# Attention, mixer and MLP in one kernel: other tiles for TensorE's transposes, the loads of K, wq and V in one place, another order behind the loop

## The chip, the cores and the metric

The kernel runs on one core of a Trainium2 chip. The metric is the device time in microseconds; lower is better. Before the change three runs gave 1611.37, 1617.12 and 1616.06 us, median 1616.06. The profile is one further execution.

## The reference

An adaptive layer norm block: modulation from `c`, attention of 32 heads against given K and V, then a mixer with an MLP. Cut to what matters (S = 2048 rows, D = 640, 32 heads of 128, F = 1728, all bf16):

```python
mod = (_silu(c) @ w_mod).reshape(c.shape[0], 6, 1, -1)
sa, ca, ga, sb, cb, gb = ...
h = _layernorm(x) * (1 + ca) + sa
q = (h @ wq).reshape(1, 2048, 32, 128).transpose(0, 2, 1, 3)
p = _softmax(einsum('bhqd,bhkd->bhqk', q, k_cache) * 128 ** -0.5)
o = einsum('bhqk,bhkd->bhqd', p, v_cache)
x = x + ga * (o.transpose(0, 2, 1, 3).reshape(1, 2048, 4096) @ wo)
h = _layernorm(x) * (1 + cb) + sb
# mixer: four column groups of the GELU, shifted by 1, -1, 2, -2 rows
t = _gelu(_layernorm(h) @ w1)
x1 = h + shifted(t) @ w2
return x + gb * (x1 + _gelu(_layernorm(x1) @ w3) @ w4)
```

## The kernel before

The kernel writes its whole program as lists of operations, one list for each engine, in the order in which the code issues them; a small class (`Prog`) works out which semaphore waits are needed from the keys that each operation reads and writes. An engine executes its list in order, so the order of the calls is the schedule. DMAs are issued from SyncE's list (and the attention output's stores from GpSimd's).

**The loop (lines 532 to 616).** One step s is one tile of 128 query rows of one head; 16 tiles a head, 32 heads, 512 steps, and 12 more to drain. In step s:

- TensorE computes QK for tile s in two halves of 1024 keys (`qk`, L286), into the PSUM tile `Sps`, and, each behind a QK half, PV in two halves for the tile eight steps back (`pv`, L299; PVD = 8).
- VectorE takes each half out of PSUM with its minimum of the negated scores (L574, into one of three buffers `negS`). GpSimd joins the two minima (L584), and ScalarE computes exp into the ring `Pb` (L587), whose ten slots hold one tile each.
- PV needs the probabilities transposed, in the ring `PTs`. For 14 of the 16 tiles SyncE does it with a DMA transpose from SBUF to SBUF (`transpose`, L222): a pair of tiles in one instruction where the pair is whole, behind the second tile's exp, else a single tile. For the two tiles in `PE_TILES` TensorE does it against an identity matrix (`t_piece`, L253), four transposes behind each PV half, and ScalarE or VectorE copies the result out of PSUM (`t_evac`, L262 and L264).
- Q of the next head is computed a little at a time (`q_piece`, L237): 20 pieces, placed by `QPIECE` in half-steps where no transpose of TensorE stands (`taken`); ScalarE copies it out (`q_evac`, L244).
- For every second tile ScalarE copies the PV result out (L565); GpSimd divides by the row sums (L440, L447) and stores groups of four tiles to DRAM (L454).

`PE_TILES` is (3, 10): tile j is transposed in steps j+3 (first half) and j+4 (second half). VectorE copies the second half of tile 3, ScalarE the other three. Pairs for the DMA are then 0,1; 4,5; 6,7; 8,9; 12,13; 14,15, and singles 2 and 11: eight transposes a head. SyncE's list also has the loads of the next head: K (`load_k`, L205, itself a DMA transpose) in step 2, wq in step 6 (L209), V in step 9 (L214). The last head loads parts of the stored attention output instead (`load_ot`, L497, a DMA transpose), in steps 2 and 9.

**Behind the loop.** `a_pe(j)` (L524) multiplies the attention output of query tile j by wo, over 32 heads; tile 0 is done in three parts, two of them in the loop's drain, ahead of the PV of the tiles at steps NG+PVD-3 and NG+PVD-2 (NG = 512). For each j VectorE then makes the residual and its norm statistics (`a_s1`), the modulated norm (`a_s2`) and the mixer's norm (`nrm_of(1, j)`), two tiles behind one another; GpSimd computes the reciprocal deviations (L624, L626). `n_t(j)` transposes the normed tile on TensorE (L665), ScalarE copies it (L668). `b_op(cc, n)` is one of five column blocks of the mixer's first matmul for 512 rows (L700) with its GELU on ScalarE (L708). `c_op(j)` is the second matmul with its residual (L742, L746). `d_op` and `e_op` are the MLP (L757, L806). `run_fill` puts operations from a list between others.

Of the kernel before, what the change touches and what calls it, by code (L numbers as in the profile page):

```python
# [115 lines left out]
def bass_adaLN_cond__mha_block_cached__mixer_s_mlp__prompt_kernel(  # L116
    nc, A_x, A_k_cache, A_v_cache, A_wq, A_wo, B_x, B_w1, B_w2, B_w3, B_w4, c, w_mod, out,
):
    _, SQ, D = A_x.shape
    _, H, SK, DH = A_k_cache.shape  # L120
    FF = B_w3.shape[1]
    assert DH == 128 and D % 128 == 0 and SQ % 512 == 0 and SK == 2048
    KT = D // 128
    NQT = SQ // 128
# [7 lines left out]
    NG = H * NQT  # L132
# [5 lines left out]
    with ExitStack() as es:  # L138
# [11 lines left out]
        if True:  # L150
            with ExitStack() as es1:
                sb1 = lambda name, shape, dt: es1.enter_context(nc.sbuf_tensor(name, shape, dt))
                RP = 10
                PVD = 8
                PE_TILES = (3, 10)
# [45 lines left out]
                G = Prog(nc, es1, "a")  # L201
# [64 lines left out]
                by_dve = lambda g, r: r == 1 and g % NQT == PE_TILES[0]  # L266

                taken = [u for j in PE_TILES for u in range(2 * (j + 3), 2 * (j + 5))]
# [247 lines left out]
                def a_pe(j, b=None, parts=(0, 1, 2)):  # L516
                    if b is None:
                        b = ybank()
                    pr, z = divmod(j, 2)

                    def f(t):
                        for c0, cw in NC2:
                            for hh in range(OTC[parts[0]], OTC[parts[-1] + 1]):
                                ins = t.matmul(YB[b][:, c0:c0 + cw], OTj[pr % 2][:, 2 * hh + z, :], wo[:, hh, c0:c0 + cw],  # L524
                                               start=(hh == 0), stop=(hh == H - 1))
# [6 lines left out]
                for s in range(NG + PVD + LAG):  # L532
# [10 lines left out]
                    for half in range(2):  # L543
                        if s < NG:
                            qk(s, half)
                        if half == 0 and s in (NG + PVD - 3, NG + PVD - 2):
                            b0 = a_pe(0, None if s == NG + PVD - 3 else b0, (s - NG - PVD + 3,))
                        if 0 <= g_ < NG:
                            pv(g_, half)
                        if s == 0 and half == 1:  # L550
                            q_head0(NQC - 1)
                        if h + 1 < H and 2 * j + half in QPIECE:
                            cc, q = QPIECE[2 * j + half]
                            q_piece(h + 1, cc, q)
# [28 lines left out]
                    if s < NG:  # L583
# [128 lines left out]
                for i in range(NQT + 1):  # L712
                    if i < NQT:
                        b = a_pe(0, b0, (2,)) if i == 0 else a_pe(i)
                        if i >= 3:
                            n_t(i - 3, i == 3)
                        if i == NQT - 3:
                            for z in range(2):
                                G.op("gpsimd", lambda g, z=z: g.memset(us[:, :, z * SQ:z * SQ + 4], 0.0), w=[("usz", z)] + OT0K)
                        if i % 2 == 1 and (i + 3) // 2 < NQT // 2:  # L720
                            load_ot((i + 3) // 2)
# [11 lines left out]
                G.dma("sync", lambda e: e.dma_start(w4[0:FL, NFT - 1, :], B_w4[(NFT - 1) * 128:FF, :]), "w4b", w=["w4b", "wo"])  # L733
                def c_op(j):
# [141 lines left out]
```

## Time and profile before

| | us |
|---|---|
| median of three runs | 1616.06 |
| lowest, highest | 1611.37, 1617.12 |
| the profiled execution, its own time | 1608.0 |
| its span (first to last instruction) | 1606.2 |
| TensorE matmuls, busy | 1488.3 (93%) |
| VectorE, busy | 1394.8 (87%) |
| ScalarE, busy | 1294.5 (81%) |
| GpSimd, busy | 625.0 (39%) |
| the DMA engines moved | 333.60 MB, mean 208 GB/s |
| mean granted clock of TensorE | 0.993 |

How to read the lines below. A line of the groups names a source line, an engine, an operation, output and input tiles with their shapes and the count; then the busy time, the mean length of one in ns, and the idle time of the engine just before them with what ended most of it. A line of the timeline gives the start in us from the span's start, the length, the engine, the source line and the count; in brackets the idle time before and its releaser. PE is TensorE's matmul, PEld its weight load, DVE VectorE, ACT ScalarE, POOL GpSimd, SP SyncE. The loop runs from about 35 to 1259 us of the span, what is behind it to 1606.2.

### The profile page before, as it was taken

To read this page: it belongs to the slowest core of one execution; us is meant where nothing else is said; L and a number is where in the kernel's file an instruction comes from. 1 tells how busy PE (TensorE), PEld (TensorE's weight loads), DVE (VectorE), ACT (ScalarE), POOL (GpSimd) and SP (SyncE) were. 2 spreads that over 40 slices of the span, in tenths; PEclk is the share of its full clock that TensorE was granted. 3 is DMA by queue.
4 is the path that set the end of the run, shared out by engine and by line. 5 is a ranking of instruction groups with operands and counts; after the bars stand their busy time and mean duration, and the time that the engine had idled before them with its cause. 6 is when DMAs were issued, how large, how long until landed. Compare 5 with 4: busy or idle time off the path is not lost.

```text
span 1606.2 us, 34619 instructions
## 1 busy us (share of the span) xinstructions
PE 1488.3 (93%) x13978; PEld 961.6 (60%) x14231; DVE 1394.8 (87%) x2463; ACT 1294.5 (81%) x1145; POOL 625.0 (39%) x1394
## 2 busy tenths in 40 slices
PE   5899999989999999899999999999999799999999
PEld 3466666666666666666666666666666555545444
DVE  6999999999999999999999999999999366656425
ACT  4999999999999999999999999999999400055330
POOL 0244444444444444444444444444444333322000
PEclk9999999999999999999999999999999899999999
DMA  9999999999999999999999999999999995430000
GB/s 308 229 229 237 236 244 236 229 234 251 231 248 247 235 244 240 229 242 237 241 246 241 240 237 233 238 237 246 236 238 241 243 214 106 106 111 1 17 17 34
DMA packets 1167936, 333.60 MB, mean 208 GB/s; under 512 B 1148384, under 2 KB 1161760, under 8 KB 1167776
## 3 DMA queue, kind: packets, MB, share of 16 engines
q1 hardware_dynamic: 1161632, 314.59, 97.1%
q0 software_dynamic: 6144, 16.79, 3.7%
q8 instruction: 112, 1.84, 0.5%
q14 instruction: 48, 0.39, 0.1%
HBM read 43.48 MB, written 19.40 MB: 39 GB/s over the span
## 4 chain that ended last, share of the span: by engine, by line
DVE 36%; PE 22%; ACT 20%; DMA 12%; issue 9%; POOL 1%; POOLq 0%; DVEq 0%
DVE negS L574 33%; ACT ring L587 16%; DMA ring<-ring 12%; PE Sps L524 9%; PE Sps L806 4%; PE Oaug L757 2%; PE QPp L757 2%; ACT ring L262 2%; PE Sps L742 1%; PE PTp L299 1%; ACT kv L244 1%; DVE ring L264 1%; ACT Of L565 1%; PE Sps L286 1%; DVE ring L364 1%
## 5 line engine op out<-in xcount | busy, mean ns | idle before, releaser
L574 DVE TENSOR_SCALAR_CACHE_REDUCE negS<-Sps 128x1024 f32<-128x1024 f32 x1024 | 1178.6, 1221 | 30.0 <-PE Sps L286 29.3
L587 ACT ACTIVATE ring<-negS,small 128x2048 bf16<-128x2048 f32 x512 | 1029.3, 2018 | 22.3 <-POOL small L584 20.7
L299 PEld LDWEIGHTS PTp<-kv,ring 128*128 128x128 bf16 x8192 | 551.9, 98 | 313.9 <-DMA ring<-ring 100.8
L299 PE MATMUL PTp<-kv,ring 128*128 128x129 bf16 x8192 | 647.5, 221 | 52.5 <-DMA ring<-ring 51.8
L286 PE MATMUL Sps<-kv 128*128 128x512 bf16 x1950 | 592.5, 381 | 35.0 <-DVE negS L574 17.2
L584 POOL TENSOR_SCALAR small<-small 128x1 f32<-128x1 f32 x512 | 146.9, 287 | 628.4 <-DVE negS L574 628.3
L286 PEld LDWEIGHTS Sps<-kv 128*128 128x128 bf16 x2048 | 143.2, 97 | 139.4 <-DVE negS L574 94.9
L447 POOL TENSOR_SCALAR On<-Of,small 128x128 bf16<-128x128 f32 x512 | 191.6, 375 | 13.0
L440 POOL TENSOR_TENSOR small<-Of,small 128x4 f32<-128x4 f32 x128 | 133.2, 1041 | 14.6 <-ACT Of L565 14.5
L668 ACT COPY kv<-PTp 128x640 bf16<-128x640 bf16 x32 | 22.0, 692 | 141.1 <-PE PTp L665 141.1
L454 POOL DMA_DIRECT2D o_scratch<-On x128 | 103.1, 806 | 40.8 <-POOL On L447 37.2
L565 ACT COPY Of<-PTp 128x259 f32<-128x259 f32 x256 | 96.2, 376 | 19.6 <-PE PTp L299 19.6
L237 PE MATMUL Oaug<-hTx,kv 128*128 128x512 bf16 x264 | 100.4, 385 | 3.7 <-DVE hTx L396 3.7
L237 PE MATMUL QPp<-hTx,kv 128*128 128x512 bf16 x259 | 97.7, 382 | 2.7 <-ACT hTx L391 2.3
L574 DVE DVE_READ_ACCUMULATOR negS<-Sps 128x1 f32 x1024 | 86.2, 84 | 0.0
L624 POOL TENSOR_SCALAR negS<-negS 128x1 f32<-128x1 f32 x48 | 24.4, 508 | 143.9 <-DVE negS L633 143.9
L638 DVE TENSOR_TENSOR ring<-Sps,mod_bc 128x640 f32<-128x640 f32 x16 | 13.2, 824 | 72.8 <-PE Sps L524 72.8
L524 PE MATMUL Sps<-wo,hTx 128*128 128x512 bf16 (+1 forms) x503 | 70.5, 300 | 0.6 <-issue 0.2
L524 PE MATMUL Sps<-wo,negS 128*128 128x512 bf16 (+1 forms) x505 | 69.3, 298 | 0.4
L810 DVE TENSOR_TENSOR ring<-Sps,ring 128x640 f32<-128x640 f32 x15 | 12.4, 824 | 62.9 <-PE Sps L806 62.8
L262 ACT COPY ring<-Oaug 128x1024 bf16<-128x1024 bf16 x64 | 65.3, 1021 | 0.0
L524 PEld LDWEIGHTS Sps<-wo,hTx 128*128 128x128 bf16 x512 | 40.1, 99 | 31.2 <-issue 1.7
(88 smaller groups left out, 1008.8 us busy)
## 6 DMA issues: line engine op xcount, KB each, us to landing
kv<-in_A_v_cache_dram SPq DMA_DIRECT2D x32, 512.0 KB, 5.0
o_scratch<-On POOLq DMA_DIRECT2D x128, 128.0 KB, 3.8
ring<-in_A_x_dram SPq DMA_DIRECT2D x8, 640.0 KB, 6.4
kv<-in_A_wq_dram SPq DMA_DIRECT2D x32, 160.0 KB, 3.4
wo<-in_A_wo_dram SPq DMA_DIRECT2D x1, 5120.0 KB, 16.4
ring<-ring SPq DMA_TRANSPOSE x256, 7.0
ring<-in_w_mod_dram SPq DMA_DIRECT2D x1, 3200.0 KB, 13.0
out_dram<-wo SPq DMA_DIRECT2D x15, 160.0 KB, 1.8
```

The source lines that it names most:

```text
L237: G.op("tensor", lambda t: t.matmul(JB[jb], wq[:, hb, q, :], hT[:, q, cc * 512:(cc + 1) * 512], start=(q == 0), stop=(q == KT - 1)), r=[(" ...
L262: G.op("scalar", lambda a: a.copy(dst, src), r=[("J", jb)], w=[("PT", g % RP, r)])
L286: ins = t.matmul(Sps[:, col:col + 512], QT[:, hb, j * 128:(j + 1) * 128], KTs[:, hb, col:col + 512], start=True, stop=True)
L299: ins = t.matmul(ob[:, 0:129], PTs[:, b, kt, :], Vaug[:, hb, kt, 0:129], start=(kt == 0), stop=(kt == NKT - 1))
L440: G.op("gpsimd", lambda g: g.tensor_tensor(out=rl[:, 4 * b:4 * b + 4], in0=Of[:].rearrange("p a z d -> p (a z) d")[:, 4 * b:4 * b + 4, 128 ...
L447: G.op("gpsimd", lambda g: g.tensor_scalar(out=On[:, b, z, :], in0=Of[:, 2 * b + z // 2, z % 2, 0:128], scalar1=rl[:, 4 * b + z:4 * b + z ...
L454: G.dma("gpsimd", lambda e: e.dma_start(o_scr[jj // 2:jj // 2 + 2, :, hh].rearrange("a p z d -> p a (z d)"), On[:, b].rearrange("p (a z) d ...
L524: ins = t.matmul(YB[b][:, c0:c0 + cw], OTj[pr % 2][:, 2 * hh + z, :], wo[:, hh, c0:c0 + cw], start=(hh == 0), stop=(hh == H - 1))
L565: G.op("scalar", lambda a, p=p: a.copy(Of[:, p % 4].rearrange("p z d -> p (z d)")[:, 0:259], PO[:, (p % 2) * 512:(p % 2) * 512 + 259]), r= ...
L574: G.op("vector", lambda v, half=half, s=s, r8=r8: v.tensor_scalar(out=negS[:, s % 3, half * 1024:(half + 1) * 1024], in0=Sps[:, half * 102 ...
L584: G.op("gpsimd", lambda g, r8=r8: g.tensor_scalar(out=nm[:, r8:r8 + 1], in0=nm0[:, r8:r8 + 1], scalar1=nm1[:, r8:r8 + 1], scalar2=None, op ...
L587: G.op("scalar", lambda a, s=s, r8=r8: a.activation(Pb[:, s % RP, :], negS[:, s % 3, :], ACT.Exp, bias=nm[:, r8:r8 + 1], scale=-1.0), r=[( ...
```

## The change

In the loop, `PE_TILES` becomes {8: 3, 9: 6}: TensorE transposes tile 8 in steps 11 and 12 and tile 9 in steps 15 and 16, the last of these being step 0 of the next head. DMA transposes are then seven whole pairs. VectorE copies the second half of tile 8 in every head and that of tile 9 in odd heads. `taken`, and so `QPIECE`, follows. K, wq and V are loaded together in step 7, behind the transpose of tiles 6 and 7; the last head's loads of attention output come in steps 5 and 7. Part 0 of the first wo tile moves one step ahead in the drain.

Behind the loop, wo's tiles 14 and 15 are each cut into four parts of eight heads, with mixer blocks and transposes between them (`a_mixed`), and the order of VectorE's work there changes: tile 15's `nrm_of(1, 15)` comes behind `c_op(0)`, its `n_t(15)` behind two more mixer blocks.

```diff
-                PE_TILES = (3, 10)
+                PE_TILES = {8: 3, 9: 6}
...
-                by_dve = lambda g, r: r == 1 and g % NQT == PE_TILES[0]
+                by_dve = lambda g, r: r == 1 and (g % NQT == 8 or g // NQT % 2 == 1)
 
-                taken = [u for j in PE_TILES for u in range(2 * (j + 3), 2 * (j + 5))]
+                taken = [u % (2 * NQT) for j, o in PE_TILES.items() for u in range(2 * (j + o), 2 * (j + o + 2))]
...
-                        if half == 0 and s in (NG + PVD - 3, NG + PVD - 2):
-                            b0 = a_pe(0, None if s == NG + PVD - 3 else b0, (s - NG - PVD + 3,))
+                        if half == 0 and s in (NG + PVD - 4, NG + PVD - 2):
+                            b0 = a_pe(0, None if s == NG + PVD - 4 else b0, ((s - NG - PVD + 4) // 2,))
...
-                            g = s - 3 - r
-                            if 0 <= g < NG and is_pe(g):
-                                t_piece(g, r, half)
-                                if half == 1:
-                                    evacs.append((t_evac, g, r))
+                            for o in PE_TILES.values():
+                                g = s - o - r
+                                if 0 <= g < NG and PE_TILES.get(g % NQT) == o:
+                                    t_piece(g, r, half)
+                                    if half == 1:
+                                        evacs.append((t_evac, g, r))
...
-                        if j == 2 and h >= 1 and h + 1 < H:
-                            load_k(h + 1)
-                        if h + 1 == H and j in (2, PVD + 1):
-                            i = 0 if j == 2 else 1
+                        if j == PVD - 1 and h + 1 < H:
+                            if h >= 1:
+                                load_k(h + 1)
+                            if h + 2 < H:
+                                load_wq(h + 2)
+                            load_v(h + 1)
+                        if h + 1 == H and j in (PVD - 3, PVD - 1):
+                            i = 0 if j == PVD - 3 else 1
                             load_ot(0, OTC[i], OTC[i + 1], i)
-                        if j == 6 and h + 2 < H:
-                            load_wq(h + 2)
-                        if j == PVD + 1 and h + 1 < H:
-                            load_v(h + 1)
...
+                def a_mixed(j, others):
+                    b = None
+                    n = len(others)
+                    for i, fs in enumerate(others):
+                        b = a_pe(j, b, hs=(H * i // n, H * (i + 1) // n))
+                        for fn, x, y in fs:
+                            fn(x, y)
+                    return b
+
-                for i in range(NQT + 1):
-                    if i < NQT:
+                for i in range(NQT):
+                    if i < NQT - 2:
                         b = a_pe(0, b0, (2,)) if i == 0 else a_pe(i)
...
                         a_s1(i, b)
-                        for n in {NQT - 2: (0, 1), NQT - 1: (2, 3, 4)}.get(i, ()):
-                            b_op(0, n)
                     if 1 <= i:
                         a_s2(i - 1)
                     if 2 <= i:
                         nrm_of(1, i - 2)
+                    if i == NQT - 2:
+                        b = a_mixed(i, [[(b_op, 0, 0)], [(b_op, 0, 1)], [(n_t, i - 3, False), (b_op, 0, 2)], [(b_op, 0, 3)]])
+                        a_s1(i, b)
+                    if i == NQT - 1:
+                        b = a_mixed(i, [[(b_op, 0, 4)], [(n_t, i - 3, False), (b_op, 1, 0)], [(b_op, 1, 1)], [(b_op, 1, 2)]])
+                        nrm_of(1, i - 1)
+                        a_s1(i, b)
+                        a_s2(i)
...
+                b_op(1, 3)
+                b_op(1, 4)
                 n_t(NQT - 3, False)
-                nrm_of(1, NQT - 1)
-                for n in range(KT):
-                    b_op(1, n)
                 n_t(NQT - 2, False)
-                n_t(NQT - 1, False)
...
                 for j in range(NQT):
                     c_op(j)
+                    if j == 0:
+                        nrm_of(1, NQT - 1)
                     if j >= 2:
                         n_t(j - 2, False)
-                    run_fill(2)
+                    run_fill(1 if j in (4, 5) else 2)
+                    if j == 0:
+                        n_t(NQT - 1, False)
```

More of the change, by code (lines that the diff above doesn't have):

```diff
@@ L514, in ybank, with a_pe @@
                     return yn[0] % 2
-                def a_pe(j, b=None, parts=(0, 1, 2)):
+                def a_pe(j, b=None, parts=(0, 1, 2), hs=None):
                     if b is None:
@@ L519, in a_pe @@
                     pr, z = divmod(j, 2)
+                    h0, h1 = hs or (OTC[parts[0]], OTC[parts[-1] + 1])
                     def f(t):
                         for c0, cw in NC2:
-                            for hh in range(OTC[parts[0]], OTC[parts[-1] + 1]):
+                            for hh in range(h0, h1):
                                 ins = t.matmul(YB[b][:, c0:c0 + cw], OTj[pr % 2][:, 2 * hh + z, :], wo[:, hh, c0:c0 + cw],
@@ L716, in bass_adaLN_cond__mha_block_cached__mixer_s_mlp__prompt_kernel @@
                             n_t(i - 3, i == 3)
[L717 to L721, printed above, removed]
+                    if i == NQT - 3:
+                        for z in range(2):
+                            G.op("gpsimd", lambda g, z=z: g.memset(us[:, :, z * SQ:z * SQ + 4], 0.0), w=[("usz", z)] + OT0K)
+                    if i % 2 == 1 and (i + 3) // 2 < NQT // 2:
+                        load_ot((i + 3) // 2)
+                    if i < NQT - 2:
                         a_s1(i, b)
-                        for n in {NQT - 2: (0, 1), NQT - 1: (2, 3, 4)}.get(i, ()):
-                            b_op(0, n)
                     if 1 <= i:
```

## The prediction

> **What bounds the kernel now.** I read the slices and the queues of the page first, then the groups of instructions, then SyncE's timeline over one head, then the timelines behind the loop.
>
> ```profile
> DMA  9999999999999999999999999999999995430000
> ...
> q1 hardware_dynamic: 1161632, 314.59, 97.1%
> ...
> L574 DVE TENSOR_SCALAR_CACHE_REDUCE negS<-Sps 128x1024 f32<-128x1024 f32 x1024 | 1178.6, 1221 | 30.0 <-PE Sps L286 29.3
> L587 ACT ACTIVATE ring<-negS,small 128x2048 bf16<-128x2048 f32 x512 | 1029.3, 2018 | 22.3 <-POOL small L584 20.7
> L299 PE MATMUL PTp<-kv,ring 128*128 128x129 bf16 x8192 | 647.5, 221 | 52.5 <-DMA ring<-ring 51.8
> ```
>
> Three resources are nearly full in the loop, and the reader is to see who waits for whom: VectorE (L574) waits for TensorE's QK, TensorE's PV (L299) waits for the transposing DMAs. In numbers per head of 16 steps: the first L574 of step 32 starts at 114.36 us, that of step 496 at 1221.14 us, so 38.16 us a head. VectorE's own need is 32 halves of 1.145 us (start to start in an undisturbed stretch) = 36.64, plus one copy L264:
>
> ```profile
> 667.04 0.69 DVE L264 COPY ring<-QPp 128x1024 bf16<-128x1024 bf16 x1
> ...
> 667.64 1.21 DVE L574 TENSOR_SCALAR_CACHE_REDUCE negS<-Sps 128x1024 f32<-128x1024 f32 x1
> ...
> 682.09 1.02 ACT L262 COPY ring<-Oaug 128x1024 bf16<-128x1024 bf16 x1
> ```
>
> The copy costs VectorE 0.60 (667.64 - 667.04), so its need is 37.24 and 0.92 us a head is waiting, some 28 us over the loop. ScalarE needs 16 exps of 1.905 start to start, 8 copies L565 of 0.26, 4 of L244 at 0.47, 3 of L262 at 0.90: 37.1. Now SyncE's timeline (start, length, line; x counts merged instructions):
>
> ```profile
> 684.82 19.82 SPq L222 DMA_TRANSPOSE ring<-ring  x5
> 704.69 3.35 SPq L205 DMA_TRANSPOSE kv<-in_A_k_cache_dram  x1
> 708.08 4.48 SPq L222 DMA_TRANSPOSE ring<-ring  x1
> 712.60 0.59 SPq L209 DMA_DIRECT2D kv<-in_A_wq_dram  x1
> 713.23 9.23 SPq L222 DMA_TRANSPOSE ring<-ring  x2
> 722.51 0.59 SPq L214 DMA_DIRECT2D kv<-in_A_v_cache_dram  x1
> ```
>
> Each row starts 0.04 us after the one before it ends: the queue never rests, and transposes start 3 to 6 us after the exp they read has ended. So the transfers set the 38.16. From landing to landing (means over 29 heads): pairs 4,5 to 14,15 take 4.11 to 4.28, pair 0,1 5.30, single tile 2 2.41, single 11 2.26, K 2.90, wq 1.28, V 3.24; sum 38.24.
>
> **The change in the loop.** *DMAs.* Singles 2 and 11 become half of pairs 2,3 and 10,11, pair 8,9 falls away. New sum: six pairs at 4.17 + 5.30 + 7.42 for the loads = 37.74, 0.5 less. The bytes stay, so the gain lies between 0 and 0.5 a head; I take 0.5 as the new capacity. By the Trainium skill, DMA: Bandwidth & Descriptors, the cost model, a DMA has a fixed part of about 2 us; if it were paid in line, one DMA fewer would give 2 us a head, 64 in all. The trace speaks against it (two singles take 4.67, a pair 4.17), so it gets no chance of its own.
>
> The loads now come behind pair 6,7. The next pair is ready four steps later (9.16 us); loads and pair take 7.42 + 4.17 = 11.59, so pair 10,11 lands 2.4 us later against its ready time than pair 6,7 does. Today a landing comes about 11 us after ready and PV starts some 0.4 after it; later pairs recover 0.4 each (4.17 in 4.58). K is wanted nine steps (20 us) and V 10 us or more behind their issue, wq a head later: these are covered. V waits for the PV of the last head's tile 15, in the same step 7, done before exp 7 ends: nothing.
>
> *Copies.* VectorE gets tile 8's second half always and tile 9's in odd heads: 1.5 copies a head for 1, +0.30 us, 16 copies x 0.60 = 9.6 us where VectorE sets the pace. ScalarE loses as many; no gain while it waits anyway.
>
> *Tile 9 is transposed late.* Its second half is transposed in step 16 and read by PV half 1 in step 17. In odd heads VectorE copies it right behind its own reduction and PV half 1 waits about 0.3 us, which TensorE makes up. In even heads ScalarE does: exp 14 starts 2.8 us after VectorE's step start (the usual least), exp 15 behind a copy L565 and one L262 at 2.8 + 1.905 - 2.29 + 0.26 + 0.90 = 3.57; the copy of step 16 ends at 3.57 + 1.905 - 2.29 + 1.02 = 4.20, that is 1.91 after step 17 starts. PV half 1 (0.46), a q piece (0.215) and QK of step 18 (0.43) follow: 3.0 to 3.15, where VectorE wants it at 2.29. That is 0.86 us on even heads. Today's steps 13 and 14 carry the same two copies and reach a lag of 4.16 instead of 3.57: the upper bound is 1.45; the lower is 0, if TensorE and VectorE stand in a DMA wait then. I take 0.86, as its inputs are rows of undisturbed steps.
>
> *QPIECE* moves to half-steps 2 to 21; a half-step with one piece takes 1.12 us of TensorE against VectorE's 1.145, and 28 of 32 carry one, before as after: nothing.
>
> *Sum.* VectorE now needs 36.64 + 1.20 = 37.84 in odd heads, 36.64 + 0.60 + 0.86 = 38.10 in even ones, mean 37.97; transfers 37.74. Two near-equal limits with noise (a pair's landing interval scatters by 0.6 to 1.0) give a little more than the larger: some 38.15. **Loop: no change**; bounds -0.4 to +0.7 us a head.
>
> **Behind the loop.** *The drain.*
>
> ```profile
> 1258.61 2.98 PE L299 MATMUL PTp<-kv,ring 128*128 128x129 bf16 x48 [0.17 <-DMA ring<-ring]
> 1266.16 1.92 PE L299 MATMUL PTp<-kv,ring 128*128 128x129 bf16 x16 [4.57 <-DMA ring<-ring]
> ...
> 1270.22 1.92 PE L299 MATMUL PTp<-kv,ring 128*128 128x129 bf16 x16 [2.15 <-DMA ring<-ring]
> ...
> 1272.36 4.32 PE L524 MATMUL Sps<-wo,hTx 128*128 128x512 bf16 x23 [0.22 <-issue]
> ```
>
> TensorE stands 4.6 and 2.2 us for tiles 11 and 12 (single 11 waited behind a load of attention output, 3.60 us of SyncE at 1256.36), and between 1264.4 and 1274.6 its granted clock is 0.50. Tile 0's projection ends at 1284.7, 25.3 us after VectorE's last reduction (1259.4, call it z). New: both loads (3.5 each) come at steps 5 and 7, nothing is between pairs 10,11 to 14,15, so 14,15 is issued at exp 15's end (z+2.8) and lands by z+9. TensorE: tiles 8 to 11 till z+4, part 0 of wo (24 matmuls, 3.4) now ahead of tile 12, tiles 12 and 13 till z+9.4, part 1 till z+12.8, tiles 14 and 15 till z+14.8, part 2 till z+17. **-8.3 us.** Bounds: -2 (only the 2.15 filled) to -10.
>
> What is late next: load_ot(1) (10.94 us of SyncE) must land for tile 2 at z+25.6; it lands at z+21 to 24. load_ot(2) comes behind xt, w1 and w2, and now lands about when tile 4 starts: +0.5 (0 to 2).
>
> *Tiles 14 and 15, the mixer.*
>
> ```profile
> 1427.08 0.45 PE L665 MATMUL PTp<-ident,Of 128*128 128x128 bf16 x5 [2.35 <-DVE Of L656]
> ...
> 1264.40:1274.60 10.20, 6.07 (x38) 4.37 (x40) 0.00 (x0) 0.38 (x1) 3.91 (x7) 0.50 1.20 282
> ...
> 1428.20:1431.60 3.40, 3.40 (x9) 1.22 (x8) 2.61 (x6) 1.21 (x3) 1.03 (x3) 0.50 0.47 100
> ```
>
> (Window rows: bounds, length, busy time by engine, clock, DMA.) Today TensorE waits 2.35 us for VectorE's norm of tile 13, smaller waits 0.7, and 3.4 us at clock 0.50 cost 1.7. The new order takes that wait away, as mixed wo and mixer work covers norms 13 and 14. But tile 15's norm now stands behind a_s1(15), a_s2(15) and c_op(0): 2.8 + 1.7 (GpSimd's rstd) + 2.0 + 1.9 + 0.7 = 9.1 us after the last wo matmul, and TensorE has 6.7 us of work till then (four mixer groups at 1.07, two transposes at 0.45, c_op 1.52): a wait of 2.4 us. If it brings the slow clock as today's 2.35 did, the gain is 0.7; if not, 2.4; if norm 15 comes in time, 4.8; if its chain is 2 us longer, -1.3. I take **-1.2**. By the Trainium skill, TensorE: Matmul & The Clock Gate, HAM oscillation, only idle gaps over some 3.4 us throttle the clock; the row here shows it after 2.35, and the measurement decides. By the rule the gain would be 2.4.
>
> The rest of the tail is TensorE at 99% busy with the same matmuls.
>
> **Sum:** 0 - 8.3 + 0.5 - 1.2 = -9 us. The profiled execution has a span of 1606.2 and a time of 1608.0 (1.8 around it), so 1599 in its terms; it is 8.1 below the median of 1616.06, and I set the difference against the median: **1607**.
>
> **Rivals.**
> - *The transfers alone set the loop (22%).* If the even heads' 0.86 falls into waits that are there anyway, 37.74 rules: -0.41 x 31 = -13, with the tail -22: 1594. For it: today's period is the queue's sum to 0.1 us. Against: VectorE alone needs 37.54.
> - *Tile 9's late copy adds to the DMA waits (22%).* Place: step 17 to 18. If the 0.92 of today stays and 0.30 + 0.43 comes on top, +0.73 x 31 = +22.6, with the tail +14: 1630, slower. It decides as soon as a head takes over 38.46 (9 us of tail over 31 heads). For it: pair 10,11 lands 2.4 us later. Against: a VectorE that stands gives the queue time to catch up.
> - *The tail gives nothing (12%).* load_ot(1) and (2) take the place of the waits: 1615.
> - My forecast, loop unchanged and tail shorter: 44%, 1602 to 1613 by itself.
>
> I call 0.5% (8 us) what can be told from no change. 1607 lies just beyond it: of my own case 26 of 44 points go to faster, with 22 of the first rival 0.48; the rest of it and the third 0.29; the second 0.22 and 0.01 of others slower. The range takes in both rivals' centres: 1592 to 1630.
>
> **What would show it.** Right: seven L222 and one stretch L205, L209, L214 a head; gaps of SyncE behind tile 7; heads of 38.0 to 38.3 us, even ones longer, with L574 waiting in step 18; no wait over 1 us at tiles 11 and 12, and part 0 at full clock; a wait of some 2 us at the transposes (L665) for norm 15. Wrong: a period under 37.8 or over 38.5, or a_pe(2) waiting for its load.

## The result and the profile after

| | before | after |
|---|---|---|
| median, us (22 runs each) | 1611.97 | 1616.24 |
| lowest, highest | 1605.56, 1620.48 | 1608.7, 1623.32 |
| the profiled execution, its time | 1608.0 | 1621.13 |
| its span | 1606.2 | 1619.3 |
| period of a head in the loop (steps 32 to 496, 29 heads) | 38.17 | 38.63 |
| end of VectorE's last reduction, z | 1259.5 | 1277.2 |
| from z to the end of the span | 346.7 | 342.2 |

The ratio is 1.0025, 95% interval 1.0014 to 1.0037: slower by 4 us, where 9 us less had been forecast. The profiled execution of before lies 4 us under its median and that of after 5 over it, so the traces differ by 13.1 us and the medians by 4.3. Two thirds of what a trace-to-trace comparison shows here is therefore scatter, up to 0.3 us a head if it all falls in the loop. The median that the forecast started from, 1616.06 of three runs, lies 4 us over that of 22. Below, traces tell where a wait sits, and the timed ratios tell what it is worth.

The page of after, its queues and groups:

```profile
q1 hardware_dynamic: 1160608, 314.58, 98.3%
...
L576 DVE TENSOR_SCALAR_CACHE_REDUCE negS<-Sps 128x1024 f32<-128x1024 f32 x1024 | 1180.1, 1219 | 38.1 <-PE Sps L286 37.5
L589 ACT ACTIVATE ring<-negS,small 128x2048 bf16<-128x2048 f32 x512 | 1018.2, 2006 | 45.2 <-POOL small L586 39.4
L299 PE MATMUL PTp<-kv,ring 128*128 128x129 bf16 x8192 | 647.1, 221 | 48.5 <-DMA ring<-ring 28.5
```

VectorE's reduction (L576, L574 of before) stands 38.1 us where it stood 30.0; PV (L299) waits less for DMAs (28.5, was 51.8), and yet the loop is longer. SyncE's timeline over one head of after:

```profile
687.10 34.23 SPq L222 DMA_TRANSPOSE ring<-ring  x7
721.37 2.18 SPq L205 DMA_TRANSPOSE kv<-in_A_k_cache_dram  x1
723.60 0.58 SPq L209 DMA_DIRECT2D kv<-in_A_wq_dram  x1
724.22 0.53 SPq L214 DMA_DIRECT2D kv<-in_A_v_cache_dram  x1
724.79 36.18 SPq L222 DMA_TRANSPOSE ring<-ring  x7
```

Seven transposes and one stretch of loads, as the diff says. But each row still starts 0.04 us after the one before it ends: the forecast had gaps behind tile 7. Over 29 heads there are four gaps of more than 0.1 us, 2.4 us in all (before: three, 1.1 us).

The waits in the loop, first of before (window 60 to 1260), then of after (60 to 1270); columns are engine, waiting line, what it waits for, us in total, times, longest. A wait of TensorE can stand in two rows, at its weight load (PEld) and at its matmul (PE):

```profile
PEld PTp L299 <- DMA ring<-ring: 93.7, 109, 2.2
...
PE PTp L299 <- DMA ring<-ring: 45.0, 68, 1.8
...
DVE negS L574 <- PE Sps L286: 23.3, 41, 1.6
```

```profile
PEld PTp L299 <- DMA ring<-ring: 54.4, 67, 2.1
...
DVE negS L576 <- PE Sps L286: 28.8, 44, 1.6
...
PE PTp L299 <- DMA ring<-ring: 24.6, 40, 1.6
...
PE PTp L299 <- ACT ring L262: 19.2, 16, 1.2
PEld PTp L299 <- DVE ring L264: 7.3, 15, 0.5
```

The last two rows are new: PV waits for the late copies of tile 9, 16 times for ScalarE's (L262), 15 times for VectorE's (L264). The waits on transposes have come down to about half, not to nothing. Per step of a head (means over 29 heads; an undisturbed step is 2.29 us, one with a VectorE copy 2.89): the late copy of an even head makes step 1 of the next head 3.28, 0.99 over; the waits on DMAs leave 0.59 a head, after 0.92 in before.

Behind the loop, TensorE's timeline of after (in brackets the idle time before the row, and its releaser):

```profile
1280.36 2.04 PE L299 MATMUL PTp<-kv,ring 128*128 128x129 bf16 x32 [0.97 <-DMA ring<-ring]
1282.25 3.42 PE L525 MATMUL Sps<-wo,hTx 128*128 128x512 bf16 x24
...
1291.57 2.05 PE L299 MATMUL PTp<-kv,ring 128*128 128x129 bf16 x32 [0.77 <-DMA ring<-ring]
...
1306.05 17.56 PE L525 MATMUL Sps<-wo,negS 128*128 128x512 bf16 x128 [1.44 <-DMA negS<-o_scratch]
...
1327.37 7.81 PE L525 MATMUL Sps<-wo,hTx 128*128 128x512 bf16 x29 [3.48 <-DMA hTx<-o_scratch]
...
1453.17 0.45 PE L667 MATMUL PTp<-ident,Of 128*128 128x128 bf16 x5 [1.33 <-DVE Of L658]
```

The 4.57 and 2.15 of before at tiles 11 and 12 are gone; 0.97 at the pair 10,11 and 0.77 at the pair 14,15 are left. Part 0 (x24, 3.42 us at full clock) stands ahead of tile 12. Below that, tile 2's projection waits 1.44 us and tile 4's 3.48 for their loads of attention output. The wait of 2.35 for tile 13's norm has become one of 1.33 for tile 15's (L658). The granted clock around the two waits (bounds, length, busy time of PE, PEld, DVE, ACT, POOL, clock, DMA share, GB/s):

```profile
1326.80:1330.20 3.40, 2.83 (x7) 1.03 (x8) 2.90 (x6) 0.00 (x0) 2.39 (x4) 0.50 1.03 222
1453.00:1460.00 7.00, 6.83 (x47) 3.76 (x48) 3.94 (x9) 4.53 (x9) 1.71 (x4) 1.00 0.95 302
```

The idle 3.48 us came with 3.4 us at half clock, the idle 1.33 us did not.

### The profile page after: what moved, and what is told of

The parts are those of the page before. It is cut to its first block, busy times and chain, and to the rows that moved or that the text cites. A ratio compares the mean times of both kernels' runs of the same rounds, so it can differ in the third digit from the quotient of the medians.

```text
span 1619.3 us, 34764 instructions
## 1 busy us (share of the span) xinstructions
PE 1508.4 (93%) x14231; PEld 971.5 (60%) x14231; DVE 1405.1 (87%) x2479; ACT 1290.5 (80%) x1129; POOL 623.9 (39%) x1394
## 4 chain that ended last, share of the span: by engine, by line
DVE 40%; PE 22%; DMA 18%; ACT 10%; issue 8%; POOL 1%; SPq 0%; DVEq 0%; POOLq 0%
DVE negS L576 36%; DMA ring<-ring 17%; ACT ring L589 8%; PE Sps L525 7%; PE Sps L825 4%; PE PTp L299 2%; PE Oaug L776 2%; PE QPp L776 2%; ACT ring L262 2%; DVE ring L264 1%; PE Sps L286 1%; PE Sps L761 1%; DMA hTx<-o_scratch 1%; DVE ring L364 1%; POOL small L586 1%
## 5 line engine op out<-in xcount | busy, mean ns | idle before, releaser
L576 DVE TENSOR_SCALAR_CACHE_REDUCE negS<-Sps 128x1024 f32<-128x1024 f32 x1024 | 1180.1, 1219 | 38.1 <-PE Sps L286 37.5
L589 ACT ACTIVATE ring<-negS,small 128x2048 bf16<-128x2048 f32 x512 | 1018.2, 2006 | 45.2 <-POOL small L586 39.4
L299 PEld LDWEIGHTS PTp<-kv,ring 128*128 128x128 bf16 x8192 | 551.8, 98 | 309.8 <-DMA ring<-ring 59.3
L299 PE MATMUL PTp<-kv,ring 128*128 128x129 bf16 x8192 | 647.1, 221 | 48.5 <-DMA ring<-ring 28.5
L286 PE MATMUL Sps<-kv 128*128 128x512 bf16 x2048 | 612.8, 381 | 33.8 <-DVE negS L576 28.3
L286 PEld LDWEIGHTS Sps<-kv 128*128 128x128 bf16 x2048 | 155.6, 97 | 147.0 <-DVE negS L576 92.4
L237 PE MATMUL Oaug<-hTx,kv 128*128 128x512 bf16 x320 | 121.6, 384 | 2.5 <-ACT hTx L391 1.6
L237 PE MATMUL QPp<-hTx,kv 128*128 128x512 bf16 x320 | 120.5, 381 | 2.5 <-ACT hTx L391 1.8
L454 POOL DMA_DIRECT2D o_scratch<-On x128 | 103.1, 806 | 40.8 <-POOL On L447 37.2
L567 ACT COPY Of<-PTp 128x259 f32<-128x259 f32 x256 | 92.4, 361 | 13.5 <-PE PTp L299 13.5
L576 DVE DVE_READ_ACCUMULATOR negS<-Sps 128x1 f32 x1024 | 84.7, 83 | 0.0
L525 PE MATMUL Sps<-wo,hTx 128*128 128x128 bf16 (+1 forms) x512 | 72.4, 302 | 3.5 <-DMA hTx<-o_scratch 3.5
L525 PE MATMUL Sps<-wo,negS 128*128 128x128 bf16 (+1 forms) x512 | 71.7, 299 | 1.4 <-DMA negS<-o_scratch 1.4
L640 DVE TENSOR_TENSOR ring<-Sps,mod_bc 128x640 f32<-128x640 f32 x16 | 13.1, 821 | 65.3 <-PE Sps L525 47.0
L262 ACT COPY ring<-Oaug 128x1024 bf16<-128x1024 bf16 x64 | 65.1, 1017 | 0.0
```

What stands on the lines that cost most here:

```text
L237: G.op("tensor", lambda t: t.matmul(JB[jb], wq[:, hb, q, :], hT[:, q, cc * 512:(cc + 1) * 512], start=(q == 0), stop=(q == KT - 1)), r=[(" ...
L262: G.op("scalar", lambda a: a.copy(dst, src), r=[("J", jb)], w=[("PT", g % RP, r)])
L286: ins = t.matmul(Sps[:, col:col + 512], QT[:, hb, j * 128:(j + 1) * 128], KTs[:, hb, col:col + 512], start=True, stop=True)
L299: ins = t.matmul(ob[:, 0:129], PTs[:, b, kt, :], Vaug[:, hb, kt, 0:129], start=(kt == 0), stop=(kt == NKT - 1))
L454: G.dma("gpsimd", lambda e: e.dma_start(o_scr[jj // 2:jj // 2 + 2, :, hh].rearrange("a p z d -> p a (z d)"), On[:, b].rearrange("p (a z) d ...
L567: G.op("scalar", lambda a, p=p: a.copy(Of[:, p % 4].rearrange("p z d -> p (z d)")[:, 0:259], PO[:, (p % 2) * 512:(p % 2) * 512 + 259]), r= ...
```

## The experiments

All ratios are to the kernel before, in runs on the same chip, with 95% intervals. "K in step 2" and the like name the step of a head in which a load is issued.

| label | edit in words | median, us | ratio | period | z to end |
|---|---|---|---|---|---|
| e1_loop_alone | after's loop and drain, old order behind | 1617.02 | 1.0033 (1.0015 to 1.0051) | 38.49 | 345.2 |
| e2_behind_alone | old loop, after's order behind | 1607.5 | 0.9972 (0.9958 to 0.9987) | 38.39 | 341.2 |
| e3_tile9_early | after, tile 9 transposed a step earlier | 1612.11 | 1.0000 (0.9985 to 1.0015) | 38.34 | 339.0 |
| e4_loads_apart | after, K, wq, V in steps 2, 6, 9 | 1603.69 | 0.9952 (0.9933 to 0.9971) | 38.13 | 342.4 |
| e5_apart_early | e4 and e3 | 1604.78 | 0.9942 (0.9923 to 0.9960) | 38.13 | 341.5 |
| e6_scalar_tile9 | e5, tile 9 all copied by ScalarE | 1602.34 | 0.9924 (0.9906 to 0.9941) | 38.20 | 340.9 |
| e7_before_stretch | before, K, wq, V together in step 7 | 1669.55 | 1.0334 (1.0312 to 1.0357) | 40.26 | 346.7 |
| e8_k_back | after, K alone back in step 2 | 1610.39 | 0.9980 (0.9965 to 0.9995) | 38.55 | 342.8 |
| e9_tail_order | after, four loads behind load_ot(2) | 1623.43 | 1.0074 (1.0051 to 1.0096) | 38.51 | 346.8 |
| e10_one_more_dma | e4, pair 10,11 as two singles | 1610.31 | 0.9994 (0.9978 to 1.0011) | 38.37 | 342.3 |
| e11_level | e6, e9's order, K in halves | 1646.52 | 1.0216 (1.0192 to 1.0240) | 39.64 | 345.9 |
| e12_k_at_5 | e6, K in step 5, wq in step 9 | 1607.38 | 0.9984 (0.9964 to 1.0004) | 38.17 | 340.0 |

Period and tail are of the one profiled execution each. Those of e1 and e8 lie 4 and 6 us over their medians and that of e12 6 under it, which is why e8's period doesn't match its ratio. Kernels with one and the same loop show the scatter: 38.17 and 38.39 (before, e2), 38.63, 38.49 and 38.51 (after, e1, e9).

### Which half loses: e1 and e2

e1 keeps the change's loop and drain and puts back what stands behind (core of the diff from after):

```diff
-                for i in range(NQT):
-                    if i < NQT - 2:
+                for i in range(NQT + 1):
+                    if i < NQT:
...
+                        for n in {NQT - 2: (0, 1), NQT - 1: (2, 3, 4)}.get(i, ()):
+                            b_op(0, n)
```

> The loop of the changed kernel (tiles 8 and 9, loads in one stretch, the drain's part 0 one step ahead) with the old order behind the loop. In the two profiles the time from the first reduction to the last grew by 17.6 us and what follows it shrank by 4.5. Theory A, the loop loses and the order behind it wins: 4 to 8 us slower than the changed kernel, so 8 to 13 us over the kernel before, a head at 38.5 to 38.7 us. Theory B, the profiles were a short and a long run and the loop costs little: within 4 us of the kernel before, a head at 38.1 to 38.3.

e2 is the reverse; the drain stays as in before too:

```diff
-                PE_TILES = {8: 3, 9: 6}
+                PE_TILES = (3, 10)
...
-                        if half == 0 and s in (NG + PVD - 4, NG + PVD - 2):
-                            b0 = a_pe(0, None if s == NG + PVD - 4 else b0, ((s - NG - PVD + 4) // 2,))
+                        if half == 0 and s in (NG + PVD - 3, NG + PVD - 2):
+                            b0 = a_pe(0, None if s == NG + PVD - 3 else b0, (s - NG - PVD + 3,))
```

> The old loop, with the changed kernel's order behind it (tiles 14 and 15 of wo mixed with mixer blocks, tile 15's norm later). Theory A: 3 to 4 us faster than the kernel before (the wait of 2.35, the two small ones and the slow clock go, a wait of 1.3 stays). Theory B: less than 1 us either way, since TensorE's work is the same and the wait only moves.

The loop with its drain costs 5.2 us (1617.02 against 1611.84), the order behind it gives 4.3 (1607.5). They add to +0.9, and the change measures +4.3; the intervals (2 to 3 us either way each) take that in. e1 falls between its two theories; e2 bears out its Theory A, if a little beyond it. So the loop, forecast at nothing, is where the time went, and the new order at the end is a gain. In the tails, the drain alone takes 1.5 us off 346.7 and the order alone 5.5: of the two parts of the tail the one forecast as large is the small one. These are single executions, though: a tail with the drain and the order of after takes from 339.0 to 342.8 us in eight kernels (after, e3 to e6, e8, e10, e12), so the drain's 1.5 isn't clear of scatter. e2's wait at the transposes is 1.32 us, for the same norm as in after.

### Is it the late copy of tile 9: e3

```diff
-                PE_TILES = {8: 3, 9: 6}
+                PE_TILES = {8: 3, 9: 5}
```

> The changed kernel with tile 9 transposed one step earlier, in steps 14 and 15, so that its second half is copied a step before PV reads it. Theory A, the late copy adds to the waits on transfers: the wait of 0.99 us in step 1 of odd heads goes, a head falls by 0.4 to 0.5 to about 38.15, 13 to 16 us less than the changed kernel. Theory B, the queue of transfers sets the period (it never rests in the changed kernel either) and the late copy only stands where a DMA wait would stand: the 0.99 goes, as much waiting comes back at other tiles, the head stays at 38.6 and the time within 4 us of the changed kernel.

1612.11 us: 4.1 less than after, where all even heads' late copies (0.99 us, 16 of them) and the 15 odd ones are gone. That is Theory B's time but for 0.1 us, though the head did fall, to 38.34. e3's waits in the loop (60 to 1260):

```profile
PEld PTp L299 <- DMA ring<-ring: 72.7, 85, 2.1
...
PE PTp L299 <- DMA ring<-ring: 33.8, 56, 1.6
```

No row for L262 or L264 is left, but TensorE's waits on transposes are 72.7 + 33.8 us where after has 54.4 + 24.6 (the same two rows). Some of the time saved in a copy is spent again at a transpose: the head isn't free to get shorter, since the transposes come late whatever TensorE does. The late copy is a real cost, but not the one that holds the loop.

### Is it the place of the loads: e4, e7, e8

e4 takes the change and puts the three loads where before has them:

```diff
-                        if j == PVD - 1 and h + 1 < H:
-                            if h >= 1:
-                                load_k(h + 1)
-                            if h + 2 < H:
-                                load_wq(h + 2)
+                        if j == 2 and h >= 1 and h + 1 < H:
+                            load_k(h + 1)
+                        if j == 6 and h + 2 < H:
+                            load_wq(h + 2)
+                        if j == PVD + 1 and h + 1 < H:
                             load_v(h + 1)
```

> The changed kernel with K, wq and V loaded in steps 2, 6 and 9 again. Theory A (copies cost the loop, the place of the loads does little): within 4 us of the changed kernel, a head at 38.5 to 38.7. Theory B (the stretch makes the transfers slower or later): 8 us or more faster than the changed kernel, a head under 38.3. Theory C (the stretch is what lowered the DMA waits from 0.92 to 0.6 a head): 8 us or more slower, a head over 38.9.

1603.69 us: 8 less than before and 12 less than after, with after's bytes and DMAs and the late copy still there. That is Theory B. e4's SyncE timeline and its waits (60 to 1260):

```profile
711.09 4.19 SPq L222 DMA_TRANSPOSE ring<-ring  x1
715.33 0.58 SPq L214 DMA_DIRECT2D kv<-in_A_v_cache_dram  x1
718.34 18.33 SPq L222 DMA_TRANSPOSE ring<-ring  x4
```

```profile
PEld PTp L299 <- DMA ring<-ring: 20.1, 28, 1.7
PE PTp L299 <- ACT ring L262: 18.2, 16, 1.2
...
PE PTp L299 <- DMA ring<-ring: 8.2, 15, 1.3
```

Between V's row (715.33 + 0.58 = 715.91) and the next pair (718.34) SyncE's queue rests 2.4 us: here the issue waits for its exp, in each of 29 heads, where in before and after a finished exp waits for its issue. Over 29 heads e4 has 68 gaps, 61.7 us, 2.1 a head; 42.6 of them stand at this place. What rests is the issuing, not the transfers: in this gap the DMA engines still have a share of 1.00, against 1.17 over 711 to 736 us (columns as in the clock's rows above):

```profile
715.91:718.34 2.43, 2.29 (x27) 1.59 (x25) 2.43 (x6) 2.43 (x3) 1.74 (x3) 1.00 1.00 225
```

From the end of its exp a pair now lands after 6.7 to 10.7 us (pair 14,15 6.71, pair 6,7 10.70); in after all seven lie between 9.65 and 11.08. The waits of PV on transposes fall from 54.4 + 24.6 to 20.1 + 8.2, while those for L262 stay at 18.2 (19.2 in after): this run parts the two causes.

e7 puts the stretch into the kernel before, whose tile 8 and 9 go through the queue as a pair right behind tile 7:

```diff
-                        if j == 2 and h >= 1 and h + 1 < H:
-                            load_k(h + 1)
+                        if j == PVD - 1 and h + 1 < H:
+                            if h >= 1:
+                                load_k(h + 1)
+                            if h + 2 < H:
+                                load_wq(h + 2)
+                            load_v(h + 1)
...
```

> The kernel before with K, wq and V loaded in one stretch in step 7, everything else old (tiles 3 and 10, six pairs and two singles). Theory A, the stretch costs by itself: 5 to 16 us slower than the kernel before, a head at 38.3 to 38.7. Theory B, the stretch costs only with the new tiles, whose pair 10,11 it delays: within 4 us of the kernel before.

1669.55 us, 55 more, over three times what Theory A allowed. Pair 8,9 lands 13.0 us after its exp, and VectorE waits for QK held behind PV; e7's waits (60 to 1322):

```profile
DVE negS L574 <- PE Sps L286: 86.9, 52, 4.1
...
PE PTp L299 <- DMA ring<-ring: 69.3, 36, 3.3
```

The waits of VectorE are 87 us where before has 23, and up to 4.1 each: the stretch by itself is a cost, and what the new tiles 8 and 9 do is to make room for it. Two things the forecast of e7 left out belong beside it. The granted clock was 0.50 in 18 stretches of its loop, 72 us in all, and in none of before's, so part of the 55 us is a slower TensorE. And its queue rests as much as e4's, 2.1 us a head, ahead of pairs 4,5 and 6,7: a rest somewhere in the head is no gain by itself, when one pair lands too late for its PV.

e8 takes K alone out of the stretch:

```diff
+                        if j == 2 and h >= 1 and h + 1 < H:
+                            load_k(h + 1)
                         if j == PVD - 1 and h + 1 < H:
-                            if h >= 1:
-                                load_k(h + 1)
```

> The changed kernel with K alone loaded in step 2 again, wq and V in step 7. Theory A, what costs is that loads and the next pair (11.6 us of transfers) do not fit into the four steps (9.2 us) behind tile 7: without K they fit (8.7 us), the queue rests again and the time comes to within 3 us of the run with all loads apart (1604). Theory B, V in step 7 instead of 9 is what costs: the time stays within 4 us of the changed kernel (1616).

1610.39 us, ratio 0.9980: by the ratios 0.45% (7 us) of the 0.73% (12 us) that e4 gets, so wq and V in step 7 still cost about 5. That is between the two theories: without K the pieces fit by Theory A's count, and yet not all of it comes back. Its queue rests 1.35 us a head, also between after's (0.08) and e4's (2.1).

### The tail: e9

In after, xt, w1 and w2 stand ahead of load_ot(2) in SyncE's queue, and tile 4's projection waits 3.48 us for it. e9 puts them behind:

```diff
-                        for cc in range(1, NQC):
-                            load_xt(cc)
+                        load_xt(1)
...
+                    if i == 1:
+                        load_xt(2)
+                        load_xt(3)
+                        G.dma("sync", lambda e: e.dma_start(w1, B_w1.rearrange("(k p) n -> p k n", p=128)), "w1", w=["w1"] + KVK)
+                        G.dma("sync", lambda e: e.dma_start(w2, B_w2.rearrange("(k p) n -> p k n", p=128)), "w2", w=["w2"] + NEG)
```

> The changed kernel with the loads of x's third and fourth part, w1 and w2 moved behind load_ot(2) in SyncE's list. Theory A, the drain's gain was given back where TensorE waits for load_ot(2) (3.5 us and the slow clock behind it, 1.7): that wait goes, 4 to 6 us less than the changed kernel, what follows the last reduction at 336 to 338 us instead of 342. Theory B, the wait moves on (to w1 before the first transposes, or to load_ot(3)): within 2 us of the changed kernel, 341 to 343 us behind the last reduction.

1623.43 us, 7 more than after, which neither theory had. The wait at tile 4 is gone, and others are there (window 1270 to 1400):

```profile
DVE ring L648 <- DMA ring<-in_A_x_dram: 15.5, 1, 15.5
...
PE PTp L664 <- DVE Of L655: 8.2, 1, 8.2
```

VectorE stands 15.5 us for x, TensorE 8.2 us behind it at the first transposes (L664), with 10.2 us at half clock after that. One engine or another waits for a load in either order; no run here takes that away.

### What a DMA costs in this queue: e10

e4 with pair 10,11 cut in two, the same bytes in one DMA more:

```diff
-                                transpose(s - 1, 2)
+                                if j == 11:
+                                    transpose(s - 1, 1)
+                                    transpose(s, 1)
+                                else:
+                                    transpose(s - 1, 2)
```

> The run with the loads apart (seven pairs, queue resting 2.1 us a head), with pair 10,11 transposed as two single tiles, one behind the other in the same step: one transfer more a head, the same bytes. Theory A, one transfer more costs what the forecast took (0.5 us): the queue rests 1.6 us or so a head, the time stays within 4 us of that run. Theory B, a transfer has a fixed cost near 2 us: the rest falls under 0.3 us a head and the time rises by 5 us or more.

1610.31 us; by the ratios 0.42% or 6.8 us over e4, 0.2 us a head. The queue's timeline in the same stretch as e4's:

```profile
721.44 0.38 SPq L214 DMA_DIRECT2D kv<-in_A_v_cache_dram  x1
721.86 20.33 SPq L222 DMA_TRANSPOSE ring<-ring  x5
```

The rest behind V is gone (0.13 us a head are left, 2.1 in e4). So both signs of Theory B came, the rest under 0.3 and 5 us or more, but its reason is not borne out. The rest goes also because a single tile 10 no longer waits for tile 11's exp. From the end of V's row to the end of tile 11's the queue takes 6.53 us in e10, 6.41 in e4 with the gap in it, and 6.76 in after, where a whole pair stands right behind V (means over 29 heads): two singles take no longer there than a pair. What can be laid at the door of one DMA more is tile 11 landing 8.37 us after its exp where the pair took 7.67, and the following pairs starting 0.4 to 0.6 later. The Trainium skill, DMA: Bandwidth & Descriptors, Anatomy of one DMA, gives a DMA a fixed part of about 2 us, measured on DMAs that GpSimd issues, and lays it mostly to its completion. The runs agree so far that no 2 us are taken from the queue; they don't show a fixed part of that size.

### Better versions: e5, e6, e11, e12

e5 is e4 with e3's line; e6 leaves VectorE tile 8 alone:

```diff
-                by_dve = lambda g, r: r == 1 and (g % NQT == 8 or g // NQT % 2 == 1)
+                by_dve = lambda g, r: r == 1 and g % NQT == 8
```

> The run with the loads apart, and tile 9 transposed in steps 14 and 15 besides. In that run SyncE's queue rested 2.1 us a head and the step 1 of odd heads still held the 0.93 us of the late copy. Theory A, VectorE sets the pace once the queue rests: the late copy's wait goes for good, odd heads fall to 37.3 and even ones to 37.9, mean 37.6, some 1589 us. Theory B, the waits on transfers come back as they did when only the tile was moved: a head at 38.0 or more, some 1600 us or above.

> As the run before it, with ScalarE copying all of tile 9 in every head, so that VectorE has one copy a head as before the change. Theory A, VectorE's copies are paid in full: another 0.3 us a head less, 37.3 to 37.4, some 1580 us. Theory B, ScalarE (37.1 us of its own a head) becomes the limit, and its lag moves to VectorE through the three buffers of negS: 37.6 or more, no gain over the run before it.

Ratios 0.9942 and 0.9924, Theory B both times (heads of 38.13 and 38.20). e6 at 1602.34 us is the fastest kernel of this study, by the ratios 12 us under before and 16 under after; it and e4 and e5 aren't told apart by their intervals. What waits are left in e6's loop sit at the pairs behind K (steps 10 to 14). e11 and e12 tried to level that, by halves of K and by another step for it (both diffs are against e6):

```diff
-                        if j == 2 and h >= 1 and h + 1 < H:
-                            load_k(h + 1)
+                        if j in (7, 11) and h >= 1 and h + 1 < H:
+                            load_k(h + 1, j // 11)
...
```

> Tile 9 early and copied by ScalarE, the order of loads behind the loop as in the first run of this set, K in two halves of 1024 keys in steps 7 and 11, V in step 9, wq in step 2. Theory A, K in step 2 is what makes pairs 2,3 to 6,7 late (waits in steps 10 to 14): these go, a head falls to 37.4 to 37.7, some 1578 to 1588 us. Theory B, ScalarE or the scatter of single transfers is the limit: a head at 38.0 or more, 1592 us or above.

```diff
-                        if j == 2 and h >= 1 and h + 1 < H:
+                        if j == 5 and h >= 1 and h + 1 < H:
                             load_k(h + 1)
-                        if j == 6 and h + 2 < H:
-                            load_wq(h + 2)
...
+                            if h + 2 < H:
+                                load_wq(h + 2)
```

> The run with tile 9 early and copied by ScalarE, with K loaded in step 5 instead of 2 and wq in step 9, behind V, instead of 6. In that run L574's counterpart still waits 0.9 us a head, in steps 10 to 14, where PV reads pairs 2,3 to 6,7, all three behind K; the four steps behind tile 7 had 1.2 us to spare. Theory A, a load delays every pair between it and the next rest of the queue: with K just ahead of pair 6,7 only that pair is late, and still in time; a head falls from 38.2 to 37.4 to 37.8, some 1585 to 1595 us. Theory B, the scatter of the pairs or ScalarE's 37.1 us a head is the limit: 38.0 or more, within 4 us of that run (1602).

Neither is faster. In e11 (1646.52 us) K's second half lands after the next head's QK wants it; waits, window 100 to 1250:

```profile
PE Sps L288 <- DMA kv<-in_A_k_cache_dram: 58.1, 29, 3.7
```

Twenty-nine heads, 2.0 us each: issued in step 11 it has 11.5 us, and stands behind a pair of 4.7. Theory B's numbers came, by a cause that neither theory named; e9's order, which cost 7 us by itself, is in e11 too. e12 (1607.38) has many heads of 37.2 us and others of 38.5 to 41.7, where pair 6,7 is late behind K: a faster head is possible, but not steadily with K there. Its profiled execution, 1601.44, is the fastest of the twelve timed, so its trace flatters it.

## Why the prediction was wrong, and where it was right

**The loop.** The step that failed is "Sum. VectorE now needs ... mean 37.97; transfers 37.74 ... some 38.15. Loop: no change". The trace shows 38.63 (38.49 and 38.51 in e1 and e9, which have the same loop), in the profile 14 us over 31 heads; by the medians (4.3, with the tail's own gain of about 4.5 taken off) the loop and its last head cost some 9. In the sum's own terms, the copies came as forecast (38.04 of VectorE), and the waits on DMAs, which were to fall from 0.92 a head to 0.18 (38.15 - 37.97), fell only to 0.59: 38.04 + 0.59 = 38.63. Of its terms:
- VectorE's need was near: each added copy took 0.60, and the even heads' late copy 0.99 instead of 0.86, at the place forecast (step 17 to 18 of its head). That makes 38.04 instead of 37.97.
- The transfers were not. "Later pairs recover 0.4 each (4.17 in 4.58)" is the part that broke. The seven pairs land 4.55 us apart in the mean (3.87 to 5.68, by the middle one of the 16 arrivals that a DMA reports), and two steps are 4.58. From the end of its exp to its landing a pair takes 11.02 (pair 10,11), 11.08, 10.01, 10.62, 9.65, 10.23 and 10.52 us (pair 6,7): what is recovered up to pair 2,3 is mostly lost again before the loads come. So pair 10,11 lands 0.5 us later than pair 6,7 against its exp, not 2.4.
- "Today's period is the queue's sum to 0.1 us", as the first rival has it, measured nothing. Intervals from landing to landing add up to the period in every kernel, whatever sets it: 38.21 for before, 38.68 after, 38.12 in e4, 40.28 in e7. So 4.17 and 37.74 were no capacity; they were the pace of the head, cut into pieces.
- The cost of the stretch was put at 2.4 us later for one pair, with the rest covered. Behind tile 7 there are four steps, 9.16 us, without a transpose. K 3.08, wq 0.68, V 3.06 and pair 10,11 4.07 take 10.9 us of landing intervals and overfill them; as these are pieces of the pace too, that is an estimate. e4 puts only V there, and its pairs catch up at that place: 10.70 us from exp to landing for pair 6,7, 7.67 for pair 10,11. After has no such place, and PV finds one transpose or another late in each head. That the place of the loads is worth 12 us is shown by e4, with e7 and e8 beside it. That it acts through how late a pair lands when PV wants it is my reading: it fits the waits of e4 and e7, but a rest in the queue is no sign of it by itself (2.1 us a head in the fast e4 and in the slow e7), and no run sets the lag alone.
- The last head takes 40.4 us, 3.3 more than before's, a term that the sum did not have (e1, e3 and e9 have it too, 40.5 to 41.8). SyncE's timeline there:

```profile
1251.49 9.45 SPq L222 DMA_TRANSPOSE ring<-ring  x2
1260.98 3.66 SPq L497 DMA_TRANSPOSE hTx<-o_scratch  x1
1264.69 5.00 SPq L222 DMA_TRANSPOSE ring<-ring  x1
1269.73 3.53 SPq L497 DMA_TRANSPOSE hTx<-o_scratch  x1
```

Two loads of 3.66 and 3.53 us stand between pairs of a queue that is already late. In e4, with a queue that rests, the last head takes 37.4.

**The rivals.** By the number "the tail gives nothing" (1615) is nearest to 1616.24, and that is luck: the tail did give some 4 us, and the loop lost 9. By the mechanism "Tile 9's late copy adds to the DMA waits" (1630) came nearest: its own test, a head over 38.46, is met, if barely (38.49 to 38.63 in three profiles), with the copy and the DMA waits (0.59 a head) both there. But e3 shows the copy worth 4 us, and e4 shows the larger price to be the stretch, which no rival named as the cause. "The transfers alone set the loop" fails with its capacity of 37.74.

**The tail.** Forecast -9, measured -4.5 in the profile; by the timed runs the order at the end alone gives 4.3 (e2).
- The drain: tile 0's projection ends at z+18.7 (before z+25.3), so -6.6 of the -8.3. Pair 14,15 was issued at z+5.8 instead of z+2.8, and landed at z+14.4 instead of z+9. e4, whose loop isn't late, issues it at z+6, so this isn't the loop's lateness; both have the two loads of attention output among the last head's pairs.
- "What is late next: +0.5" is mis-sized most: 1.44 for load_ot(1), 3.48 for load_ot(2) and 1.7 of lost clock make 6.6. This is the rival "the tail gives nothing" for the drain. e1, where the drain's gain is 1.5, shows the same waits (1.29 and 4.04 us); e9 took the longer one away and others came, so that the waits ate the drain's gain is read from the traces and not shown by a run.
- The order at the end: forecast -1.2, with a wait of 2.4 and the slow clock. The wait was 1.33 and the clock stayed at 1.00, so -5.5 by e2's tail, of which 3.4 is in these waits and the clock (2.35 + 0.7 + 1.7 - 1.33). The place and the cause (tile 15's norm) were right.

**Open** are the parts of e4's gain: how much comes from whole pairs, one DMA fewer (e10 gives at most 6.8 us to it) and tiles 8 and 9, against pairs that land earlier; why K's place alone gives e8 little more than half; and a tail without a wait for a load.

## What to carry to other kernels

A queue that never rests tells of no capacity: add up landing intervals and the period always comes out. Nor does a rest tell of spare room by itself: issuing can rest while the DMA engines go on at a share of 1.00 (e4), and a kernel whose queue rests can be the slowest (e7). Measure instead how long each transfer takes from the moment its data are ready to its landing, and against what deadline. Look where in a period late transfers can catch up, and keep such a place open when loads move; moving all loads to the place with the most room closed it here, and the gain of the rest of the change (8 us, e4) was lost with it. Where single executions scatter by more than the effect, let several timed runs of half the change, then of one line of it, say which part costs.

## What the runs showed of the hardware

- An idle of 2.35 us on TensorE was followed by 3.4 us at a granted clock of 0.50 in before, and again in e1 and e7; 1.33 us was not (after). The length of one idle doesn't decide it: 2.50 us in e8 (up to 140.7 of its span) was not followed by a slow clock, and 1.60 in e12 (up to 604.4), with 0.67 shortly before it, was. The Trainium skill, TensorE: Matmul & The Clock Gate, HAM oscillation, puts the limit at some 3.4 us of idle; these runs have the slow clock after shorter ones.
- One DMA more for the same bytes cost at most 0.2 us a head, and 0.7 us until its data landed; the queue's time from V to the end of tile 11 did not grow (6.53 us in e10, 6.76 in after).
- While SyncE issued nothing for 2.43 us, the DMA engines had a share of 1.00 (e4): a gap in the issuing is no gap in the transfers.
- Twelve executions of one kernel spanned from 8.7 us (e3) to 20 us (e12, 1601.44 to 1621.44).
